# Loading modulation weights in row-block pieces, with piecewise matvecs, tile 2 on VectorE and no-op matmuls between pieces

## The chip, the cores and the metric

The kernel runs on one core of one Trainium2 chip. Time is device microseconds of that core, several executions per kernel; the profile adds one traced execution. The engines are called as in the profile: PE (matmul), DVE (VectorE), ACT (ScalarE), POOL (GpSimd), SP (the queue that issues most transfers). "Granted clock" is the TensorE clock in the records, 1.0 being full speed.

## The reference

```
mod = (silu(c) @ w_mod).reshape(1, 6, 1, 1024)        # sa, ca, ga, sb, cb, gb
h = layernorm(x) * (1 + ca) + sa
x = x + ga * linear_attention(h, wqkv, wo)             # q, k, v = h @ wqkv, phi(k).v, ...
h = layernorm(x) * (1 + cb) + sb
x = x + gb * swiglu(h, w_gate, w_up, w_down)
```

x is 2048x1024, all weights are bf16. Before any K = h @ wk can start, the kernel needs x (row tiles of 128), their layernorm, the transposes, and sa and 1+ca: two matrix-vector products with 1024x1024 blocks of w_mod, 2 MB each. In the first 35 us, row chunk 0 (tiles 0 to 3) is prepared and its K computed.

## The kernel before

w_mod comes in two column halves ("early" = 512 columns for both shift q=0 and scale q=1, "late" = the other 512). In the kernel before each early block is one 1 MB transfer:

```python
def load_mod(b, q, lo, hi):
    nc.sync.dma_start(out=wme[b][q][:, :, lo:hi], in_=wm_v[:, :, q*D + b*NB + lo : q*D + b*NB + hi])
load_mod(0, 1, 0, NB); load_mod(0, 0, 0, NB)
load_k(0); load_k(1); load_x(3); load_k(2); load_k(3)
load_mod(1, 1, 0, NB); load_mod(1, 0, 0, NB // 2)
load_k(4); load_k(5); load_mod(1, 0, NB // 2, NB); load_k(6); load_k(7)
...
def rstd_of(mv, n):                       # on GpSimd
    ...; nc.gpsimd.tensor_tensor(out=rstd, in0=veps, in1=neg_half, op=ALU.pow)
def normalise_act(dst, src, mv, rstd):    # nmr on GpSimd, then ScalarE
    nc.gpsimd.tensor_scalar(out=nmr, in0=mean, scalar1=rstd, scalar2=-1.0, ...)
    nc.scalar.activation(out=dst, in_=src, func=ACT.Identity, bias=nmr, scale=rstd)
...
with in_order(nc.vector, nc.scalar, nc.gpsimd):       # these queues keep the order of this text
    ...
    xns = [ln1_norm(*ln1_stats(0, t)) for t in range(3)]   # stats and normalise, tile by tile
    pe_transpose_tile(hT, xns[0], 0, DC);      keep_warm(spare, 3)
    pe_transpose_tile(hT, xns[1], 1, DC);      keep_warm(spare, 2)
    mod_block(0, 1, 0, 4)                       # 32 matvecs, one column block after the other
    pe_transpose_tile(hT, xns[2], 2, DC // 2); keep_warm(spare, 4)
    for lo, hi in ((0, 1), (1, 4)):
        mod_block(0, 0, lo, hi)                 # 8 matvecs, then 24
        for cc in range(lo, hi): modulate(hT, cc, ca1T, saT, 0, H)
    k_mms(0, gs, accs, 0, 4)                    # K, columns 0 to 3, tiles 0 to 2: 24 matmuls
    xn3 = ln1_norm(*ln1_stats(0, 3), dve=True)
    pe_transpose_tile(hT, xn3, 3, DC // 2)      # copy out: half on ACT, half on DVE
    ...                                         # late w_mod, K columns 4 to 7, then V
```

A matvec is one matmul with a single moving column (N=1). `keep_warm` issues no-op matmuls (zero weights).

## Time and profile before

| kernel before | |
|---|---|
| median time | 839.24 us (839.12 to 839.3) |
| traced span, PE busy | 836.6 us, 99% |
| first K matmul (wk) | 14.50 us |
| first V matmul (wv) | 31.95 us |
| start of the last VectorE multiply | 833.52 us, that is 801.57 after the first V |

The whole kernel is bound by PE, as these lines of the profile page show (parts 1, 2 and 4: busy time with share of the span, granted clock in 40 slices, and the engines of the chain that ended last):

```profile
PE 829.8 (99%) x4701; PEld 380.7 (46%) x4701; DVE 307.6 (37%) x598; ACT 170.1 (20%) x255; POOL 60.9 (7%) x165
...
PEclk9999999999999999999999999999999999999999
...
PE 97%; DMA 1%; DVE 1%; SPq 0%; ACT 0%; issue 0%
```

The change touches only the start. These are lines of the timeline of the kernel before (start in us, duration, engine, line, operation, out<-in, count, and in brackets the idle time in front and what ended it):

```profile
5.20 0.55 POOL L199 TENSOR_TENSOR rstd<-veps,neg_half 128x1 f32<-128x1 f32 x1 [3.91 <-DVE veps L197]
...
5.85 0.26 POOL L213 TENSOR_SCALAR nmr<-mv,rstd 128x1 f32<-128x1 f32 x1
6.15 1.24 ACT L215 ACTIVATE xn<-x_sb,nmr,rstd 128x1024 bf16<-128x1024 bf16 x1 [0.38 <-POOL nmr L213]
...
6.82 0.55 POOL L199 TENSOR_TENSOR rstd<-veps,neg_half 128x1 f32<-128x1 f32 x1 [0.71 <-DVE veps L197]
...
7.66 0.61 PE L101 MATMUL tp<-ident,xn 128*128 128x128 bf16 x8
...
13.30 0.35 PE L98 MATMUL mod_ps<-scT,wme 128*128 128x1 bf16 x8 [0.69 <-DMA wme<-in_w_mod_dram]
...
14.50 5.34 PE L98 MATMUL acc<-wk,hT 128*128 128x512 bf16 x24
...
31.95 13.98 PE L98 MATMUL acc<-wv,hT 128*128 128x512 bf16 x64
```

The last thing before K is the second w_mod block, which lands at 13.25 us. Two rows of the windows view (busy us and instructions per engine in a stretch, then granted clock, DMA share and GB/s) show PE at full clock there, busy for 1.84 and 1.06 of the 2 us:

```profile
8.00:10.00 2.00, 1.84 (x18) 0.86 (x15) 1.24 (x4) 1.62 (x2) 0.81 (x2) 1.00 1.03 341
...
12.00:14.00 2.00, 1.06 (x15) 0.48 (x14) 0.70 (x3) 0.37 (x1) 0.00 (x0) 1.00 1.05 388
```

### The profile page before, as it was taken

The page shows a single profiled execution, that of the slowest core. Times are in us where ns is not written, and L with a number is a line of the kernel's source. Part 1 is how long each engine was busy: PE and PEld are TensorE (multiplying, and loading weights), DVE is VectorE, ACT ScalarE, POOL GpSimd, SP SyncE. Part 2 cuts the span into 40 slices and gives each one's busy share as a digit, 9 for nine tenths or more (in the row PEclk, how much of TensorE's full clock was granted, in tenths as well). Part 3 has the DMA queues.
Part 4 walks back from the last instruction along what each step waited for, and adds up shares of the span by engine and source line. Part 5 has one row for each costly group of instructions (what it writes and reads, how often), then busy time and mean ns, then how long its engine had stood idle before and what let it go on. Part 6 is the DMA issues. An engine that isn't in the chain of part 4 may idle for free.

```text
span 836.6 us, 11355 instructions
## 1 busy us (share of the span) xinstructions
PE 829.8 (99%) x4701; PEld 380.7 (46%) x4701; DVE 307.6 (37%) x598; ACT 170.1 (20%) x255; POOL 60.9 (7%) x165
## 2 busy tenths in 40 slices
PE   8999999999999999999999999999999999999998
PEld 4444444444444444444444444444444444444444
DVE  5755554587413324521111344222114431111122
ACT  3455343334211111101111110111110101111000
POOL 2011211111130001100000010000001100000000
PEclk9999999999999999999999999999999999999999
DMA  9894890029997446337434173672505529710011
GB/s 311 305 253 100 254 213 2 13 68 239 366 243 262 151 151 207 120 99 229 150 102 151 45 221 100 201 239 62 189 1 127 188 69 322 241 60 0 13 64 51
DMA packets 127668, 129.34 MB, mean 155 GB/s; under 512 B 33920, under 2 KB 109184, under 8 KB 127104
## 3 DMA queue, kind: packets, MB, share of 16 engines
q1 hardware_dynamic: 123568, 115.36, 45.7%
q0 software_dynamic: 4048, 13.25, 5.4%
q8 instruction: 37, 0.61, 0.3%
q14 instruction: 15, 0.12, 0.1%
HBM read 108.53 MB, written 12.72 MB: 145 GB/s over the span
## 4 chain that ended last, share of the span: by engine, by line
PE 97%; DMA 1%; DVE 1%; SPq 0%; ACT 0%; issue 0%
PE acc L98 89%; PE a_ps L98 7%; DMA wme<-in_w_mod_dram 1%; PE kvp L98 1%; PE modr L98 0%; PE den L98 0%; PE mod_ps L98 0%; DVE hT L218 0%; SPq L120 0%; DVE wo L528 0%; PE wf L98 0%; DVE pq L273 0%; ACT eb L270 0%; ACT hT L226 0%; PE tp L101 0%
## 5 line engine op out<-in xcount | busy, mean ns | idle before, releaser
L98 PE MATMUL acc<-h2T,wgu 128*128 128x512 bf16 x1792 | 387.6, 379 | 0.0
L98 PEld LDWEIGHTS <-wgu 128*128 128x128 bf16 x1792 | 175.3, 98 | 211.3
L98 PE MATMUL acc<-wd,gu 128*128 128x512 bf16 (+2 forms) x924 | 196.1, 373 | 0.0
L597 DVE TENSOR_TENSOR gu<-acc,e 128x512 bf16<-128x512 f32 x112 | 77.5, 692 | 299.2 <-PE acc L98 296.5
L596 ACT ACTIVATE e<-acc 128x512 f32<-128x512 f32 x112 | 66.9, 597 | 374.8 <-PE acc L98 374.8
L98 PEld LDWEIGHTS <-gu 128*128 128x128 bf16 x924 | 89.3, 98 | 104.4
L98 PEld LDWEIGHTS <-hT 128*128 128x128 bf16 x512 | 49.2, 98 | 60.4 <-DVE hT L218 1.5
L618 DVE TENSOR_TENSOR e<-acc,gb_bc 128x512 f32<-128x512 f32 (+2 forms) x33 | 22.3, 675 | 131.9 <-PE acc L98 131.9
L98 PE MATMUL acc<-wk,hT 128*128 128x512 bf16 x256 | 57.6, 379 | 0.8 <-DVE hT L218 0.7
L98 PE MATMUL a_ps<-wo,pq 128*128 128x512 bf16 x256 | 57.4, 379 | 0.0
L98 PE MATMUL acc<-hT,wq 128*128 128x512 bf16 x256 | 56.8, 379 | 0.0
L98 PE MATMUL acc<-wv,hT 128*128 128x512 bf16 x256 | 55.9, 379 | 0.0
L270 ACT ACTIVATE eb<-acc 128x512 bf16<-128x512 f32 x64 | 37.9, 595 | 66.2 <-PE acc L98 63.1
L215 ACT ACTIVATE xn<-x,nmr,rstd 128x1024 bf16<-128x1024 f32 x16 | 19.8, 1240 | 126.3 <-POOL nmr L213 126.3
L565 POOL DMA_DIRECT2D x_scratch<-x x16 | 9.7, 608 | 418.5 <-DVE x L558 418.5
L98 PEld LDWEIGHTS <-pq 128*128 128x128 bf16 x256 | 25.0, 98 | 30.2
L98 PEld LDWEIGHTS <-wq 128*128 128x128 bf16 x256 | 24.6, 98 | 29.8 <-issue 0.9
L271 DVE TENSOR_SCALAR eb<-eb 128x512 bf16<-128x512 bf16 x64 | 18.4, 292 | 49.0 <-ACT eb L270 49.0
L558 DVE TENSOR_TENSOR x<-a_ps,x_sb 128x512 f32<-128x512 f32 x32 | 22.1, 691 | 7.9 <-PE a_ps L98 7.8
L199 POOL TENSOR_TENSOR rstd<-veps,neg_half 128x1 f32<-128x1 f32 x32 | 17.9, 559 | 75.3 <-DVE veps L197 72.9
L308 ACT CAST v<-acc 128x512 bf16<-128x512 f32 x32 | 18.3, 582 | 23.1 <-PE acc L98 23.0
L621 DVE TENSOR_TENSOR ob<-e,x1r 128x512 bf16<-128x512 f32 (+2 forms) x33 | 22.3, 675 | 1.0
(70 smaller groups left out, 263.1 us busy)
## 6 DMA issues: line engine op xcount, KB each, us to landing
wgu<-in_B_w_gate_dram SPq DMA_DIRECT2D x28, 1024.0 KB, 7.9
wgu<-in_B_w_up_dram SPq DMA_DIRECT2D x28, 1024.0 KB, 8.7
x_sb<-in_A_x_dram SPq DMA_DIRECT2D x32, 256.0 KB, 6.8
wml<-in_w_mod_dram SPq DMA_DIRECT2D x8, 1024.0 KB, 8.7
x_scratch<-x POOLq DMA_DIRECT2D x16, 512.0 KB, 3.0
x1r<-x_scratch SPq DMA_DIRECT2D x31, 256.0 KB, 2.8
wd<-in_B_w_down_dram SPq DMA_DIRECT2D x7, 1024.0 KB, 6.0
rbc<-rden_scratch POOLq DMA_DIRECT2D x16, 256.0 KB, 5.4
```

Of the source, the lines that this page charges most:

```text
L98: return tc.keep_in_program_order(nc.tensor.matmul(out, lhsT=lhsT, rhs=rhs, start=start, stop=stop))
L199: nc.gpsimd.tensor_tensor(out=rstd[:, 0:n], in0=veps[:, 0:n], in1=neg_half[:].to_broadcast([P, n]), op=ALU.pow)
L215: nc.scalar.activation(out=dst, in_=src, func=ACT.Identity, bias=nmr[:], scale=rstd[:, 0:1])
L270: nc.scalar.activation(out=e[:], in_=acc, func=ACT.Exp)
L271: nc.vector.tensor_scalar(out=e[:], in0=e[:], scalar1=1.0, scalar2=PHI_EPS, op0=ALU.min, op1=ALU.add)
L308: nc.scalar.copy(out=v[:, t * D + nb * NB:t * D + (nb + 1) * NB], in_=acc[:])
L558: nc.vector.tensor_tensor(out=x1[:, ns], in0=a_ps[:], in1=x_t[:, ns], op=ALU.add)
L565: nc.gpsimd.dma_start(out=x1_dram[st * P:(st + 1) * P, :], in_=x1[:])
L596: nc.scalar.activation(out=sg[:], in_=ps[0][:], func=ACT.Silu)
L597: gm = nc.vector.tensor_tensor(out=guT[sc][f // GPT][:, f % GPT, :], in0=ps[1][:], in1=sg[:], op=ALU.mult)
L618: nc.vector.tensor_tensor(out=yt, in0=y_ps, in1=gb_bc[:, ns], op=ALU.mult)
L621: nc.vector.tensor_tensor(out=ob, in0=yt, in1=x1r, op=ALU.add)
```

## The change

The intent: K should start sooner after the last w_mod byte. Each w_mod block is loaded as four transfers of two row blocks (256 KB), and the matvecs of a piece accumulate as it lands, so that only 8 matvecs follow the last piece. Tile 2 is normalised on VectorE, all tile copies become one VectorE copy, and no-op matmuls stand between late pieces to keep PE's clock up. All of late w_mod now comes before wk 4 to 7. The diff, cut to its core (several statements stand on one line, the comments are added):

```diff
+    MP = 2
+    def load_mod(b, q):
+        for j in range(0, DC, MP):
+            lo = q * D + b * NB
+            nc.sync.dma_start(out=wme[b][q][:, j:j + MP, :], in_=wm_v[:, j:j + MP, lo:lo + NB])
 ...
+    load_mod(1, 1); load_mod(1, 0)
+    for cc in range(4, DC): load_k(cc)
 ...
-        xns = [ln1_norm(*ln1_stats(0, t)) for t in range(3)]
-        pe_transpose_tile(hT, xns[0], 0, DC)
 ...
+        st = [ln1_stats(0, t) for t in range(3)]
+        xn0 = ln1_norm(*st[0])
+        xn1 = ln1_norm(*st[1])
+        keep_warm(spare, 5);  mod_block(0, 1, 0)
+        keep_warm(spare, 2);  mod_block(0, 1, 1)
+        pe_transpose_tile(hT, xn0, 0)
+        xn2 = ln1_norm(*st[2], dve=True)
+        mod_block(0, 1, 2);   keep_warm(spare, 2);  mod_block(0, 1, 3)
+        pe_transpose_tile(hT, xn1, 1)
+        mod_block(0, 0, 0);   keep_warm(spare, 1);  mod_block(0, 0, 1)
+        pe_transpose_tile(hT, xn2, 2)
+        keep_warm(spare, 1);  mod_block(0, 0, 2);   keep_warm(spare, 2);  mod_block(0, 0, 3)
+        keep_warm(spare, 3);  mod_close(0)          # one copy of sa and 1+ca, then modulate, then K
 ...                                                # K columns 0 to 3, tile 3
+        mod_open(1)
+        for k in range(3): mod_block(1, 1, k)
+        keep_warm(spare, 1, False)
         k_mms(0, gs7, accs7, 0, 2)
+        mod_block(1, 1, 3); mod_block(1, 0, 0)
+        k_mms(0, gs7, accs7, 2, 4)
+        mod_block(1, 0, 1); keep_warm(spare, 1, False)
+        mod_block(1, 0, 2); keep_warm(spare, 2, False)
+        mod_block(1, 0, 3); keep_warm(spare, 3, False)
+        mod_close(1)                                # then K columns 4 to 7
```

More of the change, by code (lines that the diff above doesn't have):

```diff
@@ L128 @@
     wme = [[big("wme", [DC, NB]) for _ in range(2)] for _ in range(2)]
-    def load_mod(b, q, lo, hi):
-        nc.sync.dma_start(out=wme[b][q][:, :, lo:hi], in_=wm_v[:, :, q * D + b * NB + lo:q * D + b * NB + hi])
+    MP = 2
[3 more added lines that the diff above has]
+            nc.sync.dma_start(out=wme[b][q][:, j:j + MP, :], in_=wm_v[:, j:j + MP, lo:lo + NB])
     def load_k(cc):
         nc.sync.dma_start(out=wk[cc // 4][:, cc % 4, :], in_=wqkv_v[:, cc, D:2 * D])
-    load_mod(0, 1, 0, NB)
-    load_mod(0, 0, 0, NB)
+    load_mod(0, 1)
+    load_mod(0, 0)
     load_k(0)
@@ L142 @@
     load_k(3)
-    load_mod(1, 1, 0, NB)
-    load_mod(1, 0, 0, NB // 2)
-    load_k(4)
-    load_k(5)
-    load_mod(1, 0, NB // 2, NB)
-    load_k(6)
-    load_k(7)
+    load_mod(1, 1)
+    load_mod(1, 0)
+    for cc in range(4, DC):
+        load_k(cc)
     def load_w(view, lo, name):
@@ L167 @@
     nc.vector.memset(neg_half[:], -0.5)
+    base = const.tile([P, DC], BF16, name="base")
+    nc.vector.memset(base[:, 0:4], 0.0)
+    nc.vector.memset(base[:, 4:DC], 1.0)
     scT = const.tile([P, DC], BF16, name="scT")
     sc32 = const.tile([P, DC, 32], BF16, name="sc32")
-    saT = const.tile([P, DC], F32, name="saT")
-    ca1T = const.tile([P, DC], F32, name="ca1T")
+    sca = const.tile([P, 2, DC], F32, name="sca")
+    saT, ca1T = sca[:, 0, :], sca[:, 1, :]
     sbT = const.tile([P, DC], F32, name="sbT")
@@ L219, in modulate, with pe_transpose_tile @@
                                 scalar2=biasT[:, cc:cc + 1], op0=ALU.mult, op1=ALU.add)
-    def pe_transpose_tile(hT, xn, t, split):
+    def pe_transpose_tile(hT, xn, t):
         tp = acc_b("tp", (DC, P), BF16)
@@ L224, in pe_transpose_tile @@
             transpose(tp[:, cc, :], xn[:, cc * P:(cc + 1) * P])
-        if split < DC:
-            nc.scalar.copy(out=hT[:, split:DC, t * P:(t + 1) * P], in_=tp[:, split:DC, :])
-        nc.vector.tensor_copy(out=hT[:, 0:split, t * P:(t + 1) * P], in_=tp[:, 0:split, :])
+        nc.vector.tensor_copy(out=hT[:, :, t * P:(t + 1) * P], in_=tp[:])
     hTs = {}
@@ L251, in ln1, with mod_open, mod_block, mod_close @@
             ln1_norm(*ln1_stats(sc, t))
-    def mod_block(b, q, lo, hi):
-        for i in range(lo, hi):
-            col = q * DC + 4 * b + i
-            for j in range(DC):
-                mm(mod_ps[:, col:col + 1], lhsT=wme[b][q][:, j, i * P:(i + 1) * P],
-                   rhs=scT[:, j:j + 1], start=(j == 0), stop=(j == DC - 1))
-        cs = slice(4 * b + lo, 4 * b + hi)
-        src = mod_ps[:, q * DC + 4 * b + lo:q * DC + 4 * b + hi]
-        if q == 1:
-            nc.vector.tensor_scalar_add(out=ca1T[:, cs], in0=src, scalar1=1.0)
-        else:
-            nc.vector.tensor_copy(out=saT[:, cs], in_=src)
+    def mod_open(b):
+        mm(mod_ps[:, b * DC:(b + 1) * DC], lhsT=ident[:], rhs=base[:], start=True, stop=False)
+    def mod_block(b, q, k):
+        for j in range(k * MP, (k + 1) * MP):
+            for i in range(4):
+                col = b * DC + q * 4 + i
+                mm(mod_ps[:, col:col + 1], lhsT=wme[b][q][:, j, i * P:(i + 1) * P], rhs=scT[:, j:j + 1],
+                   start=False, stop=(q == 0 and j == DC - 1 and i == 3))
+    def mod_close(b):
+        nc.vector.tensor_copy(out=sca[:, :, 4 * b:4 * b + 4],
+                              in_=mod_ps[:, b * DC:(b + 1) * DC].rearrange("p (q i) -> p q i", q=2))
     last_phi = [None]
@@ L411, with keep_warm @@
     nc.vector.memset(sel[:], 0.0)
-    def keep_warm(acc, n):
+    def keep_warm(acc, n, alone=True):
         for _ in range(n):
-            mm(acc[:], lhsT=sel[:, 0, :], rhs=sel[:], start=True, stop=True)
+            mm(acc[:], lhsT=sel[:, 0, :], rhs=sel[:], start=alone, stop=alone)
     gs = k_groups[0:6]
@@ L419 @@
     spare = accs[5]
-    keep_warm(spare, 11)
+    keep_warm(spare, 10)
     hT = hTs[0] = big("hT", [DC, SCW])
@@ L425 @@
         mod_ps = acc_b("mod_ps")
-        mm(mod_ps[:, 0:DC], lhsT=c_sb[:], rhs=ident[0:DC, 0:DC], start=True, stop=True)
-        keep_warm(spare, 10)
-        nc.scalar.activation(out=scT[:], in_=mod_ps[:, 0:DC], func=ACT.Silu)
-        xns = [ln1_norm(*ln1_stats(0, t)) for t in range(3)]
-        pe_transpose_tile(hT, xns[0], 0, DC)
-        keep_warm(spare, 3)
-        pe_transpose_tile(hT, xns[1], 1, DC)
-        keep_warm(spare, 2)
-        mod_block(0, 1, 0, 4)
-        pe_transpose_tile(hT, xns[2], 2, DC // 2)
@@ L436 @@
-        keep_warm(spare, 4)
-        for lo, hi in ((0, 1), (1, 4)):
-            mod_block(0, 0, lo, hi)
-            for cc in range(lo, hi):
-                modulate(hT, cc, ca1T, saT, 0, H)
+        mm(mod_ps[:, 2 * DC:3 * DC], lhsT=c_sb[:], rhs=ident[0:DC, 0:DC], start=True, stop=True)
+        mod_open(0)
+        nc.scalar.activation(out=scT[:], in_=mod_ps[:, 2 * DC:3 * DC], func=ACT.Silu)
+        st = [ln1_stats(0, t) for t in range(3)]
+        xn0 = ln1_norm(*st[0])
+        xn1 = ln1_norm(*st[1])
@@ new lines @@
+        keep_warm(spare, 5)
+        mod_block(0, 1, 0)
+        keep_warm(spare, 2)
+        mod_block(0, 1, 1)
+        pe_transpose_tile(hT, xn0, 0)
+        xn2 = ln1_norm(*st[2], dve=True)
+        mod_block(0, 1, 2)
+        keep_warm(spare, 2)
+        mod_block(0, 1, 3)
+        pe_transpose_tile(hT, xn1, 1)
+        mod_block(0, 0, 0)
+        keep_warm(spare, 1)
+        mod_block(0, 0, 1)
+        pe_transpose_tile(hT, xn2, 2)
+        keep_warm(spare, 1)
+        mod_block(0, 0, 2)
@@ L441 @@
+        keep_warm(spare, 2)
+        mod_block(0, 0, 3)
+        keep_warm(spare, 3)
+        mod_close(0)
+        modulate(hT, 0, ca1T, saT, 0, P)
+        modulate(hT, 0, ca1T, saT, P, H)
+        for cc in range(1, 4):
+            modulate(hT, cc, ca1T, saT, 0, H)
         k_mms(0, gs, accs, 0, 4)
         xn3 = ln1_norm(*ln1_stats(0, 3), dve=True)
-        pe_transpose_tile(hT, xn3, 3, DC // 2)
+        pe_transpose_tile(hT, xn3, 3)
         for cc in range(4):
             modulate(hT, cc, ca1T, saT, H, SCW)
-        mod_block(1, 1, 0, 4)
+        mod_open(1)
@@ L447 @@
+        for k in range(3):
+            mod_block(1, 1, k)
+        keep_warm(spare, 1, False)
         gs7, accs7 = k_groups[6:7], [acc_b("acc")]
         k_mms(0, gs7, accs7, 0, 2)
-        for cc in (4, 5):
-            mod_block(1, 0, cc - 4, cc - 3)
-            modulate(hT, cc, ca1T, saT)
-            if cc == 4:
-                k_mms(0, gs7, accs7, 2, 4)
-        k_mms(0, gs + gs7, accs + accs7, 4, 5)
-        k_mms(0, gs[0:4], accs[0:4], 5, 6)
-        mod_block(1, 0, 2, 4)
-        for cc in (6, 7):
-            modulate(hT, cc, ca1T, saT)
@@ L459 @@
-        k_mms(0, gs[4:6] + gs7, accs[4:6] + accs7, 5, 6)
-        k_mms(0, gs + gs7, accs + accs7, 6, 8)
+        mod_block(1, 1, 3)
+        mod_block(1, 0, 0)
+        k_mms(0, gs7, accs7, 2, 4)
+        mod_block(1, 0, 1)
+        keep_warm(spare, 1, False)
+        mod_block(1, 0, 2)
+        keep_warm(spare, 2, False)
+        mod_block(1, 0, 3)
+        keep_warm(spare, 3, False)
+        mod_close(1)
+        modulate(hT, 4, ca1T, saT, 0, P)
+        modulate(hT, 4, ca1T, saT, P, SCW)
+        for cc in range(5, DC):
+            modulate(hT, cc, ca1T, saT)
@@ L461 @@
+        k_mms(0, gs + gs7, accs + accs7, 4, DC)
         gs8, accs8 = k_groups[7:8], [acc_b("acc")]
```

## The prediction

> **What bounds it.** The page shows PE 99% busy at full clock; the chain of waits is 97% PE. The change touches only the start, so the question is when the first V matmul begins: 31.95 us in the timeline. Up to there DMA runs full (windows: about 315 to 400 GB/s). The chain sits on the w_mod transfers from 2.98 to 13.25 us, then matvecs, then the K matmuls from 14.50 us.
>
> From issue plus landing times (DMA view): the third x tile lands at about 6.2 us, w_mod (0,scale) 10.2, (0,shift) 13.25, its last late half 24.3. By bytes in issue order that is 0.26 MB/us between the first two and 0.357 MB/us from 13.25 us on. I assume it holds.
>
> **Removed.** After the last early piece, one group of 8 matvecs, copy, modulate and 24 more matvecs stood before K (13.25 to 14.50). Now only 8 matvecs remain. The tile-3 eviction was ScalarE 0.58 then VectorE 0.42 in series; it becomes one copy of 0.69. Waits in PE before K column 4 go (0.71 at 21.8, about 0.4 around 22.5 and 0.2 at 23.1).
>
> **Added and moved.** Sixteen 256 KB transfers replace five big ones. Issue costs about 0.43 us each against 0.72 us of data at that pace, and eight may be outstanding (2.1 MB), so I expect no starvation. The Trainium skill ("DMA: Bandwidth & Descriptors", Rules for kernel authors) advises 1 MiB or more per DMA; the 256 KB wk loads here run at full DMA share, so I don't charge for size. Seven no-op matmuls now lie inside the K phase, 0.216 us each: 1.5 us. All of late w_mod now precedes wk 4 to 7, and K columns 4 to 7 can't start until its last piece.
>
> **Early stage.** Pieces land at about 7.2, 8.2, 9.2, 10.2, 11.0, 11.75, 12.5, 13.25. Eight matvecs (25 ns apart) to 13.6, drain 0.16, copy 0.16, modulate of 128 columns 0.31: K starts at about 14.3, as the three no-ops end. Gain 0.2 us.
>
> **Late stage.** K 0-3: 24x0.216 to 19.5; transposes 0.45; 24 matvecs 0.6; no-op 0.22; then PE waits about 0.4 for copy and modulate, to 21.2. Two K, 16 matvecs, two K, 8 matvecs, no-op, 8 matvecs, two no-ops: to 23.5. The last piece should land at about 22.8, so PE, not DMA, is late and these no-ops cost. Eight matvecs and the copy/modulate chain (0.75, against 0.65 of no-ops): 24.45. 36 K matmuls, 7.8 us: V starts at about 32.2, 0.25 us later than before.
>
> So the early gain and the faster eviction are spent on no-ops. VectorE normalising tile 2 (0.55 instead of 1.24) is off the chain.
>
> **Clock.** The skill ("TensorE: Matmul & The Clock Gate", The HAM clock gate) says that a busy window of about 3.4 us releases the full clock and an idle one takes it back. Here warm-up matmuls were issued 0.43 us apart until 4.6 us and then at 0.22. The new start idles under 0.7 us at a time, so the clock should hold.
>
> **Time.** 839.3 us, 838.4 to 840.3. Faster by over 2%: 0.01; within 2%: 0.98; slower: 0.01.
>
> **What would show it.** K's first wk matmul at 14.1 to 14.5; first V matmul at 31.8 to 32.6; PE waiting for w_mod early but not for the last late piece; the tile-3 copy a single 0.69.
>
> **What would make it wrong.** Small transfers slowing the queue (last late piece after 23.5 us); the clock dropping in the new start; or pieces landing earlier than I interpolate.

## More of the kernel before

`in_order` pins the order of each engine's instructions to the program text. `ln1_stats` ends with rstd (one over the standard deviation) on GpSimd; `ln1_norm` begins with nmr (minus the mean times rstd) on GpSimd.

GpSimd alternates rstd, nmr, rstd, ...: tile 0 can be normalised at 6.15 us, while the statistics of tile 1 still run. PE transposes it at 7.66.

## The result, and the profile after

| | before | after |
|---|---|---|
| median of 4 runs | 839.27 us (839.12 to 839.95) | 841.65 us (840.35 to 841.74) |
| first K matmul | 14.50 us | 16.66 us |
| first V matmul | 31.95 us | 34.66 us |
| first V to last VectorE multiply | 801.57 us | 801.57 us |

The ratio is 1.0023 (95% interval 1.0006 to 1.0041). Ratios are the mean time of one kernel's fast runs over that of the other's of the same rounds, so not quite the ratio of the medians quoted. The time lies outside the predicted range of 838.4 to 840.3, on the slow side. Three of the four runs have a granted clock of 0.998 (841.58 to 841.74 us), one has 1.0 (840.35 us). For the four runs of the kernel before the record gives no clock. Their 839.12 to 839.95 lie where its clock-lost runs lie on the three later chips (838.92 to 840.40; held 837.25 to 838.75), while its traced execution (838.63) held the clock. So this ratio may compare mostly clock-lost runs on both sides.

The third and last rows of the table are the useful meter: from the first V matmul to the last multiply the two executions take the same time to 0.01 us, so the whole loss between the two traces is the 2.71 us by which V starts late. The last multiply before and after:

```profile
833.52 0.29 DVE L618 TENSOR_TENSOR e<-acc,gb_bc 128x128 f32<-128x128 f32 x1 [0.41 <-PE acc L98]
...
836.23 0.29 DVE L642 TENSOR_TENSOR e<-acc,gb_bc 128x128 f32<-128x128 f32 x1 [0.41 <-PE acc L98]
```

Of the 2.71 us, 2.16 are there when K starts, where a gain of 0.2 was predicted, and 0.55 are added between K and V (18.00 us instead of 17.45).

The page after, in the same places as before:

```profile
PE 826.1 (98%) x4624; PEld 382.1 (46%) x4706; DVE 308.3 (37%) x598; ACT 167.6 (20%) x252; POOL 60.6 (7%) x164
...
PE 96%; DVE 1%; issue 1%; DMA 1%; ACT 1%; SPq 0%; POOL 0%; POOLq 0%
```

It says nothing: the shares of an 840 us span can't show 2.7 us, and part of the difference in PE is matmul records that are missing from this trace (4624 against 4706 weight loads). The timeline after says it:

```profile
5.24 0.55 POOL L203 TENSOR_TENSOR rstd<-veps,neg_half 128x1 f32<-128x1 f32 x1 [3.95 <-DVE veps L201]
...
6.86 0.55 POOL L203 TENSOR_TENSOR rstd<-veps,neg_half 128x1 f32<-128x1 f32 x1 [1.07 <-DVE veps L201]
...
8.48 0.55 POOL L203 TENSOR_TENSOR rstd<-veps,neg_half 128x1 f32<-128x1 f32 x1 [1.07 <-DVE veps L201]
...
9.02 0.50 POOL L217 TENSOR_SCALAR nmr<-mv,rstd 128x1 f32<-128x1 f32 x2
9.32 2.37 ACT L219 ACTIVATE xn<-x_sb,nmr,rstd 128x1024 bf16<-128x1024 bf16 x2 [2.76 <-DMA wme<-in_w_mod_dram]
...
10.61 0.62 PE L101 MATMUL tp<-ident,xn 128*128 128x128 bf16 x8 [2.36 <-ACT xn L219]
...
16.66 5.35 PE L98 MATMUL acc<-wk,hT 128*128 128x512 bf16 x24
...
34.66 1.67 PE L98 MATMUL acc<-wv,hT 128*128 128x512 bf16 x7
```

GpSimd now does rstd, rstd, rstd and only then nmr. The nmr of tile 0, whose inputs were there at about 5.8 us, runs at 9.02; ACT normalises tile 0 at 9.32 instead of 6.15, and PE stands still for 2.36 us before the transposes of tile 0. No line shows PE waiting for w_mod any more: the last early piece was there at about 11.9 us (an estimate, since the trace records no landing for it: the seventh piece landed at 11.2, and pieces land about 0.75 us apart), long before PE got to it at 15.63.

But the bracket of the ACT line blames something else, "DMA wme". So does the chain of waits of the kernel after:

```profile
4.52 4.82 DMA wme<-in_w_mod_dram
9.34 1.23 ACT xn L219
```

Read literally, ScalarE would wait for a w_mod piece. The list of instructions shows how that label can come about: the normalise waits for two counters, GpSimd's and the DMA counter of x tile 0. Eight DMA counters are used in turn, and the ninth transfer, the fifth w_mod piece, counts on the same one as x tile 0. The trace itself already speaks against the label: that piece was issued at 4.52 us and took 5.2 us to land (DMA view), so until about 9.7, and the normalise began before that, at 9.32, right after the nmr of tile 0 (9.02 plus half of 0.50). Which reading holds is the first question for the experiments.

The windows of the kernel after add the clock: after the stall PE runs at half clock from 12 to 14 us and partly until 16.

```profile
8.00:10.00 2.00, 0.26 (x9) 0.17 (x7) 0.36 (x2) 0.68 (x1) 1.03 (x3) 1.00 1.06 366
10.00:12.00 2.00, 1.31 (x27) 1.15 (x29) 0.73 (x2) 1.98 (x3) 0.00 (x0) 0.98 1.08 372
12.00:14.00 2.00, 2.00 (x32) 1.72 (x30) 1.11 (x2) 0.99 (x1) 0.00 (x0) 0.50 1.06 391
14.00:16.00 2.00, 1.83 (x25) 1.34 (x25) 0.69 (x1) 0.00 (x0) 0.00 (x0) 0.67 1.08 356
```

Read in steps of 0.1 us, the windows show half clock from 11.9 to 15.3 us, a stretch of 3.4 us. The later traces show stretches of the same length (e5 once, e2 twice) or of twice that (e7, e12). Half clock for 3.4 us costs 1.7 us where PE is the limit (an estimate), and 1.7 of 838 us is what lowers the mean clock to 0.998. The traces fit: 0.998 with one stretch (the kernel after, e5), 0.996 with two or the double one (e2, e7).

Theory P: the order on GpSimd delays tile 0, and the idle PE then loses its clock. Rival W: ScalarE waits for the w_mod piece. Rival S: the small transfers or the no-ops are what costs. Rival C: the clock is lost through the interleaved matvecs, not through the gap.

### The profile page after: what moved, and what is told of

Its sections match the earlier page's. It is cut to its first block, busy times and chain, and to the rows that moved or that the text cites. A ratio compares the mean times of both kernels' runs of the same rounds, so it can differ in the third digit from the quotient of the medians.

```text
span 839.6 us, 11291 instructions
## 1 busy us (share of the span) xinstructions
PE 826.1 (98%) x4624; PEld 382.1 (46%) x4706; DVE 308.3 (37%) x598; ACT 167.6 (20%) x252; POOL 60.6 (7%) x164
## 3 DMA queue, kind: packets, MB, share of 16 engines
q0 software_dynamic: 4048, 13.25, 5.3%
## 4 chain that ended last, share of the span: by engine, by line
PE 96%; DVE 1%; issue 1%; DMA 1%; ACT 1%; SPq 0%; POOL 0%; POOLq 0%
PE acc L98 87%; PE a_ps L98 7%; DMA wme<-in_w_mod_dram 1%; PE kvp L98 1%; PE modr L98 0%; DVE stats L209 0%; PE tp L101 0%; ACT xn L219 0%; PE mod_ps L98 0%; PE den L98 0%; SPq L135 0%; SPq L120 0%; DVE wo L552 0%; PE wf L98 0%; ACT eb L273 0%
## 5 line engine op out<-in xcount | busy, mean ns | idle before, releaser
L203 POOL TENSOR_TENSOR rstd<-veps,neg_half 128x1 f32<-128x1 f32 x32 | 17.9, 558 | 78.4 <-DVE veps L201 76.1
```

The lines of the kernel that those rows point to most:

```text
L203: nc.gpsimd.tensor_tensor(out=rstd[:, 0:n], in0=veps[:, 0:n], in1=neg_half[:].to_broadcast([P, n]), op=ALU.pow)
```

## The experiments

Three groups of four kernels, each group on one chip beside its own runs of the kernel before. All gave correct results. The table lists the traced execution's K and V starts (us), and the mean time in us and the number of the runs with the clock held and of those with it lost.

| run | K | V | runs, clock held | runs, clock lost | ratio (95%) |
|---|---|---|---|---|---|
| before, 1st group | | | 837.86 (5) | 839.59 (2) | |
| e1_pool_order | 13.28 | 31.30 | 838.71 (4) | none | 1.0009 (0.9993 to 1.0026) |
| e2_before_stats_first | 17.32 | 36.13 | 840.00 (2) | 842.17 (2) | 1.0036 (1.0018 to 1.0054) |
| e3_gap_filled | 15.51 | 33.5 | 840.31 (4, one of 0.999) | none | 1.0027 (1.0012 to 1.0041) |
| e4_before_early_pieces | 14.07 | 31.51 | 838.12 (4) | none | 1.0000 (0.9986 to 1.0015) |
| before, 2nd group | | | 838.06 (5) | 840.00 (2) | |
| e5_no_late_noops | 12.99 | 32.91 | none | 840.70 (4) | 1.0027 (1.0003 to 1.0051) |
| e6_late_as_before | 13.94 | 31.09 | 838.55 (2) | 840.70 (2) | 1.0011 (0.9990 to 1.0032) |
| e7_whole_loads | 18.45 | 36.45 | 841.10 (1) | 841.81 (3) | 1.0035 (1.0015 to 1.0055) |
| e8_before_again | 13.44 | 30.88 | 837.71 (2) | 839.28 (2) | 0.9998 (0.9979 to 1.0016) |
| before, 3rd group | | | 837.96 (5) | 839.71 (6) | |
| e9_tile2_scalar | 13.44 | 31.44 | 838.44 (4) | none | 0.9995 (0.9980 to 1.0010) |
| e10_before_filled | 15.11 | 33.04 | 838.29 (6) | none | 0.9993 (0.9979 to 1.0008) |
| e11_late_filled | 13.04 | 31.20 | 838.03 (6) | none | 0.9990 (0.9976 to 1.0003) |
| e12_after_again | 17.85 | 35.84 | 840.21 (2) | 841.90 (4) | 1.0029 (1.0015 to 1.0044) |

### e1_pool_order: mend the order on GpSimd

```diff
-        st = [ln1_stats(0, t) for t in range(3)]
-        xn0 = ln1_norm(*st[0])
-        xn1 = ln1_norm(*st[1])
+        xn0 = ln1_norm(*ln1_stats(0, 0))
+        xn1 = ln1_norm(*ln1_stats(0, 1))
+        st2 = ln1_stats(0, 2)
```

> The changed kernel, with tile 0 and tile 1 each normalised right after their own statistics, so that GpSimd computes the negated scaled mean (nmr) of tile 0 before the rstd of tiles 1 and 2. Theory P (queue order on GpSimd delays the ScalarE normalise of tile 0): that normalise starts at about 6.9 us instead of 9.32, PE's 2.36 us wait before the first transposes goes, the clock stays at 1.0, the first K matmul starts at about 12.8 us (16.66 in the changed kernel, 14.50 before), the first V matmul at about 31.1, time about 838.5 us (837.8 to 839.2). Rival W (the profile's own attribution: ScalarE waits for a w_mod transfer): the normalise still starts at 9.3 and the time stays at about 841.6. Rival S (small transfers or the no-op matmuls are what costs): K starts early but the time stays above 840.5.

Lines of its timeline:

```profile
5.93 0.27 POOL L217 TENSOR_SCALAR nmr<-mv,rstd 128x1 f32<-128x1 f32 x1
6.23 1.24 ACT L219 ACTIVATE xn<-x_sb,nmr,rstd 128x1024 bf16<-128x1024 bf16 x1
6.91 0.55 POOL L203 TENSOR_TENSOR rstd<-veps,neg_half 128x1 f32<-128x1 f32 x1 [0.71 <-DVE veps L201]
...
8.09 0.61 PE L101 MATMUL tp<-ident,xn 128*128 128x128 bf16 x8
...
13.28 5.35 PE L98 MATMUL acc<-wk,hT 128*128 128x512 bf16 x24
...
31.30 4.05 PE L98 MATMUL acc<-wv,hT 128*128 128x512 bf16 x17
```

The normalise starts at 6.23 us with the w_mod transfers as they were, so it never waited for one: rival W is out, and the label in the trace of the kernel after was a wrong guess between two counters. K starts 3.4 us earlier than in the kernel after, V 3.36 earlier, and the clock stays at 1.0 in all four runs. The time, 838.68 us median, is not told apart from the kernel before on that chip by the interval. Rival S is out as the explanation of the loss: the small transfers and all no-ops are still in this kernel. With the clock held on both sides, though, e1 lies 0.85 us above the kernel before (838.71 against 837.86) and e9 0.48 us above its own (838.44 against 837.96). So the change with its order mended shows no gain in time.

### e2_before_stats_first: put only that order into the kernel before

```diff
-        xns = [ln1_norm(*ln1_stats(0, t)) for t in range(3)]
+        st = [ln1_stats(0, t) for t in range(3)]
+        xns = [ln1_norm(*s) for s in st]
```

> The kernel before, with only one thing of the change: the statistics of tiles 0 to 2 are all emitted before the first normalise, so GpSimd does rstd, rstd, rstd, nmr, nmr, nmr. Theory P: the normalise of tile 0 starts at about 9.2 us instead of 6.15, the transposes of tile 0 at about 10.5 instead of 7.66, the first K matmul at 15.4 to 16.5 instead of 14.50, time 840.2 (clock held) to 841.5 (clock lost in the 2.7 us gap). Rival W or S (needs the small transfers): no change, 839.2.

One line of text, with the large transfers and without a single new no-op, makes the kernel before lose 2.1 us with the clock held (840.00 against 837.86) and more with it lost. In its timeline the normalise starts at 9.41 us, and here, where the ninth transfer is another one, the profile names the right releaser:

```profile
9.11 0.73 POOL L213 TENSOR_SCALAR nmr<-mv,rstd 128x1 f32<-128x1 f32 x3
9.41 3.50 ACT L215 ACTIVATE xn<-x_sb,nmr,rstd 128x1024 bf16<-128x1024 bf16 x3 [3.37 <-POOL nmr L213]
10.71 0.62 PE L101 MATMUL tp<-ident,xn 128*128 128x128 bf16 x8 [2.61 <-ACT xn L215]
...
17.32 5.34 PE L98 MATMUL acc<-wk,hT 128*128 128x512 bf16 x23
```

K at 17.32 was later than the 15.4 to 16.5 that I expected, and so was the slowest run (843.0). The windows show why: this execution lost the clock from 12 to past 15 us, and a second time after 24 us, in the old late stage:

```profile
12.00:14.00 2.00, 2.00 (x29) 1.44 (x28) 0.75 (x2) 0.92 (x1) 0.00 (x0) 0.50 1.05 394
...
24.00:26.00 2.00, 1.06 (x11) 0.61 (x13) 1.50 (x8) 1.03 (x1) 0.00 (x0) 0.90 1.05 389
26.00:28.00 2.00, 2.00 (x14) 0.85 (x13) 0.88 (x3) 0.00 (x0) 0.00 (x0) 0.50 1.06 389
```

### e3_gap_filled: keep the order, fill the gap

```diff
+        keep_warm(spare, 11)
         pe_transpose_tile(hT, xn0, 0)
```

> The changed kernel with 11 more no-op matmuls (11 x 0.216 = 2.4 us) where PE waits for the first transposes (8.26 to 10.61 us). Theory P with a clock part: the wait itself stays, so K still starts late, but the clock stays at 1.0 from 10 to 16 us (0.50 and 0.67 in the changed kernel), the first K matmul starts at about 15.4 instead of 16.66, time 840.3 as in the one run of the changed kernel with granted clock 1.0 (840.35), and in every round. Rival C (the N=1 matvecs interleaved with few no-ops let the clock drop whatever stands in the gap): clock below 0.8 somewhere from 10 to 16 us and 841.6.

The no-ops, the start of K, and one row of the windows:

```profile
8.22 2.54 PE L98 MATMUL acc<-sel 128*128 128x512 bf16 x11
...
15.51 5.35 PE L98 MATMUL acc<-wk,hT 128*128 128x512 bf16 x24
...
12.00:14.00 2.00, 2.00 (x50) 1.76 (x49) 1.49 (x4) 1.20 (x1) 0.00 (x0) 1.00 1.04 387
```

As expected: K at 15.51, V at about 33.5, the windows show 1.00 throughout, and the four runs lie at 839.97 to 840.51, like the clock-held runs of the changed kernel (840.35; 840.20 and 840.21 in e12). The normalise of tile 0 starts at 9.53 us, and with the same transfers as in the kernel after, the profile here puts its wait down to nmr (3.37 us). Rival C is out: the same interleaved matvecs and no-ops hold the clock once the gap is filled. This splits the 3.36 us between the kernel after and e1: 1.2 are the clock (34.66 to 33.5), 2.2 are the wait itself (33.5 to 31.30). By the means of the runs with the clock held, the wait is 1.6 us (840.31 against 838.71). The changed kernel itself held the clock in 3 of its 10 runs; what decides this from run to run is not shown, since none of those three was traced.

### e4_before_early_pieces: only the small early transfers

```diff
-    load_mod(0, 1, 0, NB)
-    load_mod(0, 0, 0, NB)
+    for q in (1, 0):
+        for j in range(0, DC, 2):
+            nc.sync.dma_start(out=wme[0][q][:, j:j + 2, :], in_=wm_v[:, j:j + 2, q * D:q * D + NB])
```

> The kernel before, with only the two early w_mod transfers split into four pieces each of two row blocks; every other order as before. My prediction assumed that the landing time is set by bytes in issue order, so that the last early piece lands at 13.25 us either way. Theory L (pieces land earlier, as the changed kernel's trace suggests: about 11.6 us): the wait of PE for w_mod at 12.6 to 13.3 goes, the first K matmul starts at about 13.3 us instead of 14.50, the first V matmul at about 30.8 instead of 31.95, time about 838.0 us. Rival B (bytes alone): last piece at 13.2, K at 14.5, time 839.2.

K at 14.07 and V at 31.51, neither theory's numbers; the time is that of the kernel before. The last early piece landed at about 12.2 us (the seventh at 11.5, plus 0.75), 1.0 before the 13.25 of my profile of before. But e8 answers what that means: the kernel before, unchanged, had its second 1 MB block at about 11.7 us in another execution (issue at 2.98, 8.7 to landing), e2 at 12.4, e7 at 13.4 and e10 at 13.9, while the last of the small pieces landed, estimated in the same way, between 11.9 (after) and 12.8 (e6). The spread between executions is larger than any difference between 1 MB and 256 KB, so a gain or loss by size alone is not shown.

### e5_no_late_noops: take the seven late no-ops out of e1

```diff
-        keep_warm(spare, 1, False)      # and the three others: 1 + 1 + 2 + 3 no-ops
```

> The kernel e1_pool_order without the seven no-op matmuls of the late stage (7 x 0.216 = 1.5 us of PE time). First V matmul in e1: 31.30 us, first K matmul 13.28. Theory N (my prediction: PE, not DMA, is late there, so the no-ops lie on the chain): V at about 30.0 to 30.4, time about 1.0 us under e1. Rival D (the last late w_mod piece, landing at about 22.4 us in e1, is the limit and the no-ops only fill the wait for it): PE now waits for w_mod up to about 22.4, V at 31.0 to 31.3, no gain.

```profile
21.87 0.35 PE L98 MATMUL mod_ps<-scT,wme 128*128 128x1 bf16 x8 [0.31 <-DMA wme<-in_w_mod_dram]
22.59 0.35 PE L98 MATMUL mod_ps<-scT,wme 128*128 128x1 bf16 x8 [0.37 <-DMA wme<-in_w_mod_dram]
23.56 9.51 PE L98 MATMUL acc<-wk,hT 128*128 128x512 bf16 x35 [0.61 <-DVE hT L222]
```

Rival D was right: without the no-ops PE waits for the w_mod pieces, and K column 4 starts at 23.56 (23.52 in e1; the last piece lands at 22.5 in both). So the no-ops cost nothing once K starts early. And they do something: without them the clock falls, in all four runs (0.997 or 0.998), and V comes 1.6 us later. The windows of this kernel:

```profile
20.00:22.00 2.00, 1.63 (x32) 1.12 (x34) 0.55 (x3) 0.00 (x0) 0.00 (x0) 1.00 1.07 375
22.00:24.00 2.00, 1.01 (x18) 0.56 (x17) 0.98 (x4) 0.00 (x0) 0.00 (x0) 0.84 1.06 388
24.00:26.00 2.00, 2.00 (x6) 0.72 (x5) 0.76 (x3) 0.00 (x0) 0.00 (x0) 0.50 1.05 388
```

### e6_late_as_before: new early stage, old late stage

```diff
-    load_mod(1, 1); load_mod(1, 0); wk 4 to 7; piecewise late matvecs; seven no-ops
+    the loads, matvecs and K matmuls of the kernel before from late w_mod on
```

> The kernel e1_pool_order with the late stage (second half of w_mod: its three loads, their place among the wk loads, its matvecs by column block, no no-ops) as in the kernel before; the early stage stays new. First K to first V matmul was 17.45 us before and 18.02 in e1. Theory R (the new late stage is what costs, the new early stage what gains): K at about 13.3, K to V 17.45 again, V at about 30.7, about 0.6 us under e1 and 1.2 under the kernel before. Rival: the older late stage needs data that are not there 1.2 us earlier (second half of the last w_mod block at about 24.1), PE waits for w_mod and V stays at 31.3.

(The edit above is told in words; the starting point is e1.) K to V took 17.15 us (18.02 in e1), as theory R said, with the single copy of tile 3 as the likely 0.3 under the 17.45 of before. But K began at 13.94, since early pieces landed later in this execution, and two of four runs lost the clock. No gain over the kernel before is shown.

### e7_whole_loads: e1 with 1 MB transfers

```diff
-        for j in range(0, DC, MP):
-            lo = q * D + b * NB
-            nc.sync.dma_start(out=wme[b][q][:, j:j + MP, :], in_=wm_v[:, j:j + MP, lo:lo + NB])
+        lo = q * D + b * NB
+        nc.sync.dma_start(out=wme[b][q][:], in_=wm_v[:, :, lo:lo + NB])
```

> The kernel e1_pool_order with each w_mod block again loaded by one transfer of 1024 KB; the matvecs stay piece by piece. Theory L: PE in the new order waits for the whole first block (10.2 us before) and then for the whole second (13.25 us), so K starts at 15.5 to 16.2 instead of 13.28, V at about 33.5 to 34, time 2 to 2.5 us above e1. Rival (the order of the matvecs, not the size of the loads, brings K forward): K at 13.3 to 14.0 and no loss.

PE waited 2.87 us for the whole first block at 10.48, lost the clock, and K came at 18.45, later than I expected since I had not counted the clock. So the new order of matvecs needs the small transfers. That the pair of them brings K forward against the kernel before is likely but not shown: with both, and the order mended, K starts at 12.99 to 13.94 in five traces, in the two traces of the kernel before at 13.44 and 14.50.

### e8_before_again: the kernel before, with a profile

No edit.

> The kernel before, unchanged, as a control on this chip with its own profile. Expected: K at 14.5 and V at 31.95 us within 0.5, from first V to the last VectorE instruction 801.57 us as in every trace so far; same time as the kernel before beside it. It also shows whether its own start loses the clock in some runs (granted clock 0.998 in two of seven on the last chip).

K at 13.44 and V at 30.88: 1.06 us earlier than in the first profile of the same kernel, outside the 0.5 that I allowed, and all of it before K (K to V is 17.44 again). From V to the last multiply it is 801.57 us. The start of one kernel moves by a microsecond with the landing of its transfers, so single traces of two kernels must be compared by what PE waits for, not by 0.5 us of V. Two of these four runs lost the clock; over all three groups it is 12 of 29 runs of the kernel before, at 1.6 to 1.9 us each by the means in the table.

### e9_tile2_scalar: tile 2 back on ScalarE

```diff
-        st2 = ln1_stats(0, 2)
-        xn2 = ln1_norm(*st2, dve=True)
+        xn2 = ln1_norm(*ln1_stats(0, 2))
```

> The kernel e1_pool_order with row tile 2 normalised on ScalarE again (1.24 us behind tile 1 there) instead of on VectorE (0.55). Theory: in e1 the transposes of tile 2 come at 10.96 us behind the matvecs that wait for a w_mod piece, and ScalarE would have tile 2 done at about 10.4 us, so this part of the change is off the chain: K and V as in e1 (13.3 and 31.3) within the spread of the landing times (about 0.5), same time. Rival (the move to VectorE matters): transposes of tile 2 wait for ScalarE, K later by 0.3 us or more with such a wait in the trace.

K at 13.44, V at 31.44, no wait of PE for ScalarE. The move to VectorE, for which the statistics were pulled forward, gains nothing measurable.

### e10_before_filled and e11_late_filled: no-ops where the old late stage is thin

```diff
         mod_block(1, 1, 0, 4)                        # mod_cols in e11
+        keep_warm(spare, 1, False)
         k_mms(0, gs7, accs7, 0, 2)
+        keep_warm(spare, 2, False)
```

e10 is the kernel before with this and the single VectorE copy of tile 3; e11 is e6 with this.

> The kernel before with two parts of the change's late stage alone: the copy of tile 3 in one piece on VectorE (0.69 instead of 0.58 + 0.42 in series), and three no-op matmuls where PE waits at about 20.5 and 22 us. Theory H (the start of the kernel before loses the clock in about a third of its runs, 6 of 18 on the last two chips, because between the first 24 K matmuls and K column 4 too little PE work runs; no-ops there hold it): granted clock 1.0 in all six runs, K to V 17.15 to 17.3 instead of 17.45, mean of its runs 0.4 to 0.8 us under the mean of the kernel before. Rival (the clock is lost elsewhere in the start, or at random): 0.998 in some runs again and no more than 0.2 us gained.

> The kernel e6_late_as_before (new early stage with the GpSimd order mended, old late stage) with the same three no-op matmuls at about 20.5 and 22 us. e6 lost the clock in two of four runs (0.998, 0.997), e1 with its late no-ops in none of four. Theory H: clock 1.0 in all six runs, K to V about 17.2, time 0.3 to 0.8 us under the kernel before. Rival: the clock is lost in the early stage (PE waits for w_mod pieces), so some runs show 0.998 again.

The clock was 1.0 in 12 of 12 runs, beside 5 of 11 for the kernel before on the same chip. This supports theory H: the old late stage is where the kernel before tends to lose it (and the trace of e2 shows a loss exactly there; no trace of the unchanged kernel caught one). It is not proof: e4, with the old late stage and no no-ops in it, held the clock in four of four runs. The expected 17.15 to 17.3 us from K to V were not met: 17.93 and 18.16, because the late w_mod block landed late in both traced executions (waits of 0.82 and 1.04 us). The medians, 837.79 and 837.93, are about 1 us under the 838.92 of the kernel before, but both intervals contain 1, so a version that beats both kernels is likely and not proven; against the changed kernel on the same chip (841.60) the 3.7 us of e11 are clear.

### e12_after_again: the changed kernel as a control

No edit.

> The changed kernel, unchanged, as a control beside the three others on one chip. Expected: ScalarE normalises tile 0 at about 9.3 us, K starts at 15.5 (clock held) to 16.8 (clock lost), V 18.0 later, from V to the last VectorE multiply 801.57 us, clock 0.998 in most of six runs, time 2.0 to 3.5 us above the held-clock runs of the kernel before.

ScalarE normalises at 9.31, the clock is lost in four of six runs, V to the last multiply is 801.58 us, median 841.60. K at 17.85 in the traced execution is later than expected because that one was the worst (0.995, half clock from 10 to past 16 us). The loss holds on another chip.

## Why the prediction was wrong, point by point

- **The step that failed**: "VectorE normalising tile 2 (0.55 instead of 1.24) is off the chain." It is (e9), but I costed only the operation that moved. To move it, the text emits all three statistics first, and that moved rstd of tiles 1 and 2 in front of nmr of tile 0 on GpSimd. The instruction order of each engine was there to be read before the run: rstd three times, then nmr twice. I had read VectorE's and ScalarE's. The Trainium skill ("TensorE: Matmul & The Clock Gate", the table at its head) calls the queue of GpSimd, as of ScalarE and VectorE, strict first in, first out; this trace agrees, an nmr that could run at 5.8 us stands until 9.02. Cost: 2.2 us in the traces (e1 against e3), 1.6 us by the means.
- **"The new start idles under 0.7 us at a time, so the clock should hold."** The idle time was wrong: it was 2.36 us, the clock fell in 7 of 10 runs, and with the gap filled it held in four of four (e3). The rule behind it, that short gaps hold the clock, was not right either: in e5 the clock fell in all four runs, and its trace has no gap above 0.61 us there. Of the 3.4 us window that the prediction quotes, the traces show the length, in the stretches of half clock; but in the 3.4 us before the fall in the kernel after (8.5 to 11.9) PE stood idle for only 2.2 us, so a whole idle window was not needed. Cost: 1.2 us in the traces (e3 against the kernel after), 1.7 us by the means of e12.
- **"K starts at about 14.3."** The missing term is the one above; the others were pessimistic. The pieces landed up to 1.3 us earlier than I interpolated (the seventh at 11.2 instead of 12.5), and with the order mended K starts at 13.28. I had treated one landing time, 13.25, as a constant; between executions it moves from about 11.7 (e8) to 13.9 (e10) for the same 1 MB transfer.
- **"PE, not DMA, is late and these no-ops cost"**: right for the kernel as it ran, where K was so late that PE never waited for late w_mod, and K to V took 18.00 us against my 17.9 (14.3 to 32.2). That e1 takes 18.02 as well, while it waits for a piece, is luck. Wrong as a judgement of the no-ops: with K on time PE waits for the pieces, the no-ops fill that wait and hold the clock (e5).
- **Small transfers not slowing the queue, and the tail after V unchanged**: as predicted; e4 has the time of the kernel before, and V to the end is 801.57 us in both. The class, within 2%, was right as well.
- **The sum**: e1 minus before in the first traces is -0.65 us of V (31.30 against 31.95), order +2.2, clock +1.2, together +2.7 as measured. Only the last two are firm; the -0.65 is within the spread of landings, and by time e1 and the kernel before are not told apart, and with like clock e1 is the slower by 0.85 us.

## What to carry to other kernels

When a change lifts one operation forward, list the order on every in-order engine that its inputs pass through, small GpSimd steps too: a 0.26 us instruction behind two that are not needed yet held up the whole core. A releaser in a trace is a guess where an instruction waits for more than one counter; test it by moving one of the two. No-op matmuls that fill a wait for data can be worth more than they look, because they keep the clock for the real matmuls that follow.

## What the Trainium skill lacked or had wrong

- "TensorE: Matmul & The Clock Gate", Why this matters for your kernels, advises to avoid PE-idle gaps above about 3 us. Here the clock fell with shorter ones: with a 2.36 us gap (three of four runs of the kernel after; in the trace of e12, with a gap of 2.13 us, it fell at 10.1, about 1.6 us after the gap began), and in e5 in all four runs, with no gap above 0.61 us in its trace, in a stretch of N=1 matvecs, transposes and short waits (PE busy 1.63 and 1.01 us of 2.0 from 20 to 24 us). The page has no figure, also where it treats short idles, for how little work in a window still holds the clock; seven no-op matmuls over about 4 us held it in all four runs of e1.
- "DMA: Bandwidth & Descriptors", Rules for kernel authors, gives 1 MiB or more per DMA for the most bandwidth. With up to eight 256 KB transfers outstanding no loss was seen here (372 and 391 GB/s in the two windows from 10 to 14 us in the kernel after, 385 and 388 in the kernel before). Where the matvecs are ordered by piece, pieces let PE start sooner: K came at 18.45 us with 1 MB transfers (e7, with the clock lost), at 13.28 with pieces (e1). In the old order of matvecs no gain from pieces was shown (e4).
- The same page gives no spread for the time to landing. The same 1 MB transfer, issued at 2.98 us, took from 8.7 (e8) to 10.9 us (e10) in different executions.
- None of the pages that I read on traces says that DMA counters which are used in turn can make a profile name the wrong releaser: "DMA wme" for 2.76 us in the kernel after, where the wait was for GpSimd (e1) and the piece landed only at about 9.7 us, after the normalise had begun at 9.32.
